# A fused state-space and convolution kernel: two turned tiles moved to ScalarE, five steps reordered, and the last tile read in halves

## The chip, the cores and the metric

The kernel runs on one core of a Trainium2 chip. A core has five engines with an instruction queue each: TensorE (PE in the profile; its weight loads are PEld), VectorE (DVE), ScalarE (ACT), GpSimd (POOL) and SyncE (SP), which here only issues DMAs. GpSimd issues the accumulating DMAs ("sums"). The metric is the device time of one execution in microseconds. Before the change the median of three runs is 385.52 us (384.85 to 386.91); the profiled execution took 384.57 us.

## The reference

The output is g * a + (1 - g) * b for 2048 rows and 1024 columns, with a gate g for each row.

```
g = sigmoid((x * gate_w).sum(-1))
# a: a diagonal complex state space, P = 1024 states
dt = exp(log_dt);  Lam_bar = exp(dt * Lam)
Bu = einsum("bld,pd->blp", x, ((Lam_bar - 1) / Lam)[:, None] * Bmat)
h[t] = Lam_bar * h[t - 1] + Bu[t]
a = 2 * einsum("blp,dp->bld", h, Cmat).real + x * Dskip
# b: a 4-tap filter on k, times v, then a causal convolution over all 2048 rows, by FFT
kv = shift_filter(k, shift_k) * v
b = x * (causal_conv(kv, ssm_k) + kv * ssm_D)
```

## The kernel before, in words

All instructions of an engine stay in the order in which the Python code issues them (put, line 92), so the text of the kernel is the schedule of each queue. Generators are used to interleave: a step of a generator issues its next few instructions on all engines, and the code below the definitions decides when each step comes. Nearly every operation is recorded under line 94, the line of put, so instructions are told apart by the tiles that they write and read.

The work has two halves. First the convolution b, in eight blocks of 128 channels: filter taps by matmuls (taps, line 562), a forward transform of the kernel (fwd_K, 628, tiles psk to Kh or BT) and of the data (fwd_V, 651, psv to Vh) by matmuls with cosine and sine tables, products on VectorE (products, 664; tiles G, wkh, t), and an inverse transform (inverse, 716, psz to cv) that is stored to DRAM (cv_scr). PSUM is a pool of four tiles of two banks each (line 81), and ScalarE evacuates most of them. The inverse tables SI and CI are made from angles: inverse_angles (378) on VectorE, then inverse_table (389), which is an Abs and two Sin on ScalarE. The rates of the states are made by state_params (411): its second step computes abv, rv (an Exp on ScalarE), thn and nthn; its third step the small tiles up to invden; its fourth step needs Sin. Exp and Sin lie in different tables of ScalarE, and each change shows as an ACT_TABLE_LOAD. Lines 1077 to 1120 order this start.

Second the state space a, in four blocks of 512 rows (tb) and four groups of 256 states (g). Bu (783) multiplies x by B (PE tile both, odd or even), ScalarE evacuates it to U, turn_U (872) adds a rotated part by a scaling on ScalarE (tile Q) and a sum by DMA (U<-Q), scan (891) runs the recurrence on VectorE, and Cy_g (1010) multiplies the states hb and U by C into the PSUM tile psy, eight matmuls for a row tile and group. B and C come transposed by DMA (load_BT 245, load_CT 1124), x too (load_xT 250, two halves of 0.5 MB).

C has eight tiles CT[0] to CT[7] of 128 states. Each must be turned by complex factors (turn_C, 1274): two scalings of the swapped parts on ScalarE (into m or, for tiles 4 and 5, into two tiles of the pool Q), two scalings in place, and the sum of both. For tiles 0 and 1 all four scalings are on ScalarE and the sum is two accumulating DMAs; for 4 and 5 the in-place scalings are on VectorE and the sums are DMAs (CT<-Q); for 2, 3, 6 and 7 the sum too is on VectorE. The pool Q has four buffers (line 1337), shared by turn_C and turn_U: a buffer is free again when its sum has landed.

Lines 1382 to 1480 are the schedule of the second half, in sixteen steps j, one for each scan: plan[j] names the units of matmuls that follow scan j ("B9 B10", "C0" and so on). In Bu_next (1365) after each of a unit's two B tiles up to two entries of the list on_act are stepped as fillers; they hold steps of turn_C:

```
for t in turning[2 * j:2 * j + 2]:
    run(t)
on_act += [lambda t=t: step(t) for t in turning[2 * j + 2:2 * j + 4] for _ in range(2)]
```

At j = 1 run finishes tiles 2 and 3 before the fillers that were put in for them at j = 0 are used, and B9 and B10 then have eight places for fillers: four that do nothing and four for tiles 4 and 5. At the end of step 1 scale_b (999) makes row tile 0's share of b on ScalarE (pbb, gd) and sums them by DMA; it needs the loads of row tile 0 (loads, 978) and the row Dskip (rows_).

The transposed loads of the second half are issued by SP in this order: CT[0], BT(2), CT[1], CT[2] (lines 1241 to 1248), BT(3), CT[3] (1295 to 1297), x's last block (1327, into the buffer that block 0 had, so behind the matmuls of Bu(7)), the stores of the last inverse, CT[4], CT[5], loads(0), the row Dskip, CT[6], CT[7], loads(1), loads(2) (1346 to 1353).

The end is lines 1482 to 1500: the last four row tiles get their last group's matmuls one after another, and finish (1043) scales each by the gate, adds xr and stores it. For the last row tile Cy_g sorts its eight matmuls by half, and finish reads and stores it in two halves on VectorE, both behind the eight.

Of the kernel before, what the change touches and what calls it, by code (L numbers as in the profile page):

```python
# [20 lines left out]
def kernel(  # L21
# [985 lines left out]
        act(gd, rows_, func=ACT.Identity, scale=gcols[:, t_:t_ + 1])  # L1007
        gather(pbb, gd)

    def Cy_g(tb, tl, ps, g, last):  # L1010
        X = hbs[tb, g] if tl < 2 else Us[tb, g][1]
        tsl = slice(tl % 2 * 128, tl % 2 * 128 + 128)
        steps_ = [(j, c, dh) for j in range(2) for c in range(2) for dh in range(2)]
        if tb * 4 + tl == NT - 1:
            steps_.sort(key=lambda s_: s_[2])
        for j, c, dh in steps_:
            mm(ps[dh], X[:, c, j, tsl], CT[2 * g + j][:, c, dh * 512:(dh + 1) * 512],
               g == 0 and j == 0 and c == 0, last and j == 1 and c == 1)

# [23 lines left out]
    def finish(t_, ps=None):  # L1043

        rows = rows_of(of, t_)
        product(t_)
        xr = ios.pop(t_)[1]
        if ps is None:
            yield
            ga = gas.pop(t_)  # L1050
            tt(ga, ga, xr, ALU.add)
        else:
            yield
            ga = a_room(t_)
            for o, i in ps:
                put("dve", V.scalar_tensor_tensor, out=ga[:, o], in0=i, scalar=gcols[:, t_:t_ + 1], in1=xr[:, o],
                    op0=ALU.mult, op1=ALU.add)
                if len(ps) > 1:
                    move(rows[:, o], ga[:, o])
            if len(ps) > 1:  # L1060
                return
        move(rows, ga)


    def step(gen):
        next(gen, None)

    def run(gen):
        for _ in gen:
            pass  # L1070
# [27 lines left out]
    step(sp)  # L1098
    run(first)
    dg1 = dgs(1, True)  # L1100
    run(angles)
    load("kT", 1)
    load("v", 1)
    load("kn", 1)
    fwd_K(0, (0, 1))
    fwd_V(0, (0, 1))
    step(sp)
    step(turns)
    taps(1, dg1)
    step(sp)  # L1110
    step(turns)
    p0 = products(0, 0)
    steps(p0, 3)
    tv = times_v(1)
# [17 lines left out]
    for c in range(NC - 1):  # L1132
        n, nn = c + 1, c + 2
        if c == 0:
            load("kn", 2)
            load("kT", 2)
            load("v", 2)
            load_BT(0, 0)
            load_xT(0, (0,))
            p1 = products(0, 1)  # L1140
            fwd_K(n, (0, 1))
            step(p0)
            run(tv)
            dg = dgs(nn, True)
            steps(p1, 2)
            step(p0)
            step(p1)
            run(p0)
            taps(nn, dg)
            step(sp)  # L1150
            fwd_K(n, (2, 3))
            step(p1)
            step(sp)
            fwd_V(n)
            run(p1)
            run(fold_K(nn))
            tv = times_v(nn)
            step(tv)
            load("kn", 3)
            load("kT", 3)  # L1160
            load_BT(0, 1)
            apart = spread(3)
            step(apart)
            load_xT(0, (1,))
            run(apart)
            lam_diag(0, lam_pool, True)
            continue
        if c == 6:
            put("pool", nc.gpsimd.tensor_copy, stamp, xTs[2][:, 0, 0:HB + 1:HB])
        tabs, back, prod = turn_table(c - 1) if c <= NG else none, inverse(c - 1), products(c)  # L1170
        step(old)
        step(tabs)
        if c == 6:
            step(parts)
        step(back)
        step(tv)
        steps(prod, 3)
        run(tv)
        step(old)
        step(tabs)  # L1180
        run(back)
        run(old)
        fk = none
        if nn < NC:
            dg = dgs(nn)
            if by_channel(nn):
                fk = fold_columns(nn)
                step(fk)
        if c == 2:
            step(parts)  # L1190
        fwd_K(n, (0, 1))
        if c in (2, 6):
            step(parts)
        fwd_K(n, (2, 3))
        if c == 4:
            step(parts)
        if c == 6:
            run(sp)
            s5p["Q"] = s5p["wu"]
            run(turns_U[2])  # L1200
            gate(0)
        step(prod)
        if nn < NC:
            if not by_channel(nn):
                fk = mirror_K(nn)
            step(fk)
            if c < 5:
                step(fk)
            if c == 4:
                step(parts)  # L1210
            if c == 1:
                load_BT(1, 0, True)
            elif c < 5:
                load("v", nn, True)
            step(parts)
            taps(nn, dg)
            if c == 5:
                load("v", nn)
                load_xT(2, held=True)
            if nn + 1 < NC:  # L1220
                load("kT", nn + 1, True)
                load("kn", nn + 1)
                apart = spread(nn + 1)
                step(apart)
                if c == 1:
                    load_BT(1, 1)
                elif c in (2, 3):
                    load_xT(1, (3 - c,))
                run(apart)
        step(prod)  # L1230
        run(fk)
        if n == NC - 1:
            overlap_K(n)
        run(prod)
        if nn < NC:
            tv = times_v(nn)
            step(tv)
            step(parts)
        else:
            run(next(tiles))  # L1240
            for pi in range(3):
                CT[pi] = ld.tile([128, 2, D], BF16, name="CTa", tag="ld")
                if pi == 0:
                    hold(CT[0][:, 0, 0:1])
                load_CT(pi)
                if pi == 0:
                    load_BT(2, 0)
                    load_BT(2, 1)
            run(next(tiles))
            run(next(tiles))  # L1250
        fwd_V(n, (0, 1))
        if c < 6 and c != 4:
            step(parts)
            if c in (1, 3):
                step(parts)
        fwd_V(n, (2, 3))
        if c in (4, 5):
            step(parts)
        if c == 1:
            lam_diag(1, lam_pool)  # L1260
        old = tabs
# [12 lines left out]
    def turn_C(pi):  # L1274
        by_sum = pi in (0, 1, 4, 5)
        if pi in (4, 5):
            m = [s5p["Q"].tile([128, D], BF16, name="Q") for c in range(2)]
        else:
            whole_m = m_pool.tile([128, 2, D], BF16, name="m")
            m = [whole_m[:, c] for c in range(2)]  # L1280
        for c in range(2):
            act(m[c], CT[pi][:, 1 - c], func=ACT.Identity, scale=mc2i[:, pi:pi + 1])
            yield
        for c, f in enumerate((c2r, mc2r)):
            if pi < 2:
                act(CT[pi][:, c], CT[pi][:, c], func=ACT.Identity, scale=f[:, pi:pi + 1])
            else:
                ts(CT[pi][:, c], CT[pi][:, c], f[:, pi:pi + 1], None, ALU.mult)
            if by_sum:
                gather(CT[pi][:, c], m[c])  # L1290
        if not by_sum:
            tt(CT[pi], CT[pi], whole_m, ALU.add)

    turning = [turn_C(pi) for pi in range(NP)]
    load_BT(3, 0)
    load_BT(3, 1)
    load_CT(3)
    with tc.tile_pool(name="fin", bufs=1, side="right") as fin:

        count = iter(range(16))  # L1300

        def room(shape, dt, name):
            return fin.tile(shape, dt, name=name, tag=f"fin{next(count)}")

        prod, back = products(c, 0, room, False), inverse(c - 1)
        run(old)
        steps(prod, 3)
        run(turns_U[3])
        run(next(tiles))
        steps(turning[0], 2)  # L1310
        step(back)
        steps(turning[1], 2)
        run(back)
        gate(1)
        gate(2)
        steps(prod, 2)
        b6, b7 = Bu(6)
        run(b6)
        run(b7)
        run(turns_U[6])  # L1320
        run(turning[0])
        run(turning[1])
        run(prod)
        b8, b9 = Bu(7)
        run(b8)
        run(b9)
        load_xT(3)
        b10, b11 = Bu(8)
        run(b10)
        run(b11)  # L1330
# [14 lines left out]
    CT_pool(range(4, NP), "ctb")  # L1345
    load_CT(4)
    load_CT(5)
    loads(0)
    move(rows_, bc(A_Dskip.rearrange("(o d) -> o d", o=1), [128, D]))
    load_CT(6)  # L1350
# [82 lines left out]
    for j in range(NS):  # L1433
# [6 lines left out]
        advance(j)  # L1440
        for t in turning[2 * j:2 * j + 2]:
            run(t)
        on_act += [lambda t=t: step(t) for t in turning[2 * j + 2:2 * j + 4] for _ in range(2)]
        turn = turns_U[turned[j]] if j in turned else none
        if j != 10 and plan[j][0:1] != "G":
            step(turn)
# [47 lines left out]
        fins.append(finish(t0 + tl, None if tl == 1 else pss[tl][1]))  # L1494
        step(fins[tl])
    for tl in range(4):
        Cy_g(tb, tl, pss[tl][0], NG - 1, True)
        if tl == 1:
            scale_a(t0 + tl, pss[tl][1])
        run(fins[tl])  # L1500
# [28 lines left out]
```

## Time and profile before

| | |
|---|---|
| median of the runs | 385.52 us (384.85 to 386.91) |
| profiled execution | 384.57 us |
| its span, first to last instruction | 382.8 us |
| TensorE clock granted | 0.998 |
| ScalarE busy | 303.6 us (79%) |
| transposing and plain DMA queue (q1) | 45.64 MB, 55.4% of the 16 DMA engines |
| queue of the sums (q0) | 25.17 MB, 38.9% |

Times in the profile are microseconds from the start of the span. A row of a timeline gives the start, the time, the engine, the line, the operation, the tiles out<-in, the shapes and the count; in brackets stands how long the engine was idle before it and what ended that. The sums by stretch give the length of the stretch, then busy time and number of instructions of PE, PEld, DVE, ACT and POOL, the granted clock, the DMA engines' mean busy share and GB/s. A row of the chain of waits gives a start, a time and the work (or DMA, or "issue") that the later work waited for.

### The profile page before, as it was taken

What the parts mean: (1) busy time and instruction counts of PE and PEld (TensorE: products, weight loads), DVE (VectorE), ACT (ScalarE), POOL (GpSimd) and SP (SyncE); (2) the same over time, 40 slices, a digit from 0 to 9 for tenths busy, and PEclk for the clock granted to TensorE, in tenths of its full rate; (3) what the DMA queues carried; (4) which work ended last, traced back from release to release, by engine and by line L of the source; (5) the groups of instructions that cost most, each with busy time, mean ns of one, the idle gap of its engine ahead of it and who ended that gap; (6) DMA issues with size and microseconds to landing.
All of it is one profiled execution on the core that took longest, in us unless ns stands there. A gap on an engine that the chain in (4) does not pass through costs nothing.

```text
span 382.8 us, 6633 instructions
## 1 busy us (share of the span) xinstructions
PE 371.3 (97%) x2419; PEld 198.3 (52%) x2453; DVE 371.2 (97%) x599; ACT 303.6 (79%) x469; POOL 81.8 (21%) x108
## 2 busy tenths in 40 slices
PE   7899999999999999999999999989999999999995
PEld 5566458575584846744454444434444444444442
DVE  7999999999999999999999999999999999999996
ACT  5898998988979999786979699675989759937601
POOL 4011030020301102031003110413414323634100
PEclk9999999999999999999999999999999999999999
DMA  7979999998999997959999999986899999898903
GB/s 166 165 108 223 218 205 205 245 203 211 201 164 211 208 213 169 198 125 154 192 221 164 226 203 250 213 153 125 150 222 192 208 245 246 136 250 156 238 8 110
DMA packets 126402, 71.77 MB, mean 187 GB/s; under 512 B 104665, under 2 KB 107489, under 8 KB 126370
## 3 DMA queue, kind: packets, MB, share of 16 engines
q1 hardware_dynamic: 111232, 45.64, 55.4%
q0 software_dynamic: 12976, 25.17, 38.9%
q10 hardware_dynamic: 2162, 0.54, 0.8%
q8 instruction: 19, 0.31, 0.3%
q14 instruction: 13, 0.11, 0.1%
HBM read 15.48 MB, written 8.39 MB: 62 GB/s over the span
## 4 chain that ended last, share of the span: by engine, by line
PE 52%; DVE 30%; issue 9%; DMA 4%; ACT 3%; ACTq 1%; POOL 0%; DVEq 0%; POOLq 0%
PE psy L94 29%; PE both L94 15%; DVE BT L94 11%; DVE wkh L94 8%; DVE G L94 5%; DVE t L94 3%; PE psz L94 2%; DVE ks L94 2%; PE psk L94 2%; DMA CT<-Q 2%; DMA pbb<-cv_scr 1%; PE psv L94 1%; DMA rows<-in_gate_w_dram 1%; PE p L94 1%; PE taps L94 1%
## 5 line engine op out<-in xcount | busy, mean ns | idle before, releaser
L94 PEld LDWEIGHTS <-BT 128*128 128x128 bf16 x640 | 62.0, 98 | 48.3 <-issue 0.2
L94 PE MATMUL both<-xT,BT 128*128 128x512 bf16 x375 | 83.0, 379 | 0.4
L94 POOL DMA_DIRECT2D U<-Q x26 | 26.7, 1039 | 88.8 <-ACT Q L94 31.0
L94 PEld LDWEIGHTS <-hb 128*128 128x128 bf16 x256 | 24.9, 98 | 31.4 <-issue 1.6
L94 PEld LDWEIGHTS <-U 128*128 128x128 bf16 x240 | 23.5, 98 | 28.3
L94 PE MATMUL psy<-CT,hb 128*128 128x512 bf16 x157 | 36.3, 379 | 0.1
L94 ACT ACTIVATE Vh<-psv 128x1024 bf16<-128x1024 f32 x32 | 30.7, 1034 | 5.3 <-PE psv L94 5.3
L94 PE MATMUL psy<-CT,U 128*128 128x512 bf16 x149 | 34.6, 379 | 0.2
L94 ACT ACTIVATE Q<-U,lam 128x512 bf16<-128x512 bf16 (+1 forms) x52 | 29.9, 612 | 4.9 <-DMA CT<-Q 4.9
L94 DVE TENSOR_TENSOR_SCAN W<-rv,init,A 128x256 bf16<-128x256 f32 x48 | 32.2, 730 | 0.0
L94 POOL DMA_DIRECT2D G<-wkh x8 | 9.7, 1218 | 102.8 <-DVE wkh L94 102.8
L94 ACT ACTIVATE U<-both 128x512 bf16<-128x512 f32 x44 | 24.1, 595 | 8.0 <-PE both L94 7.5
L94 PEld LDWEIGHTS <-SF 128*128 128x128 bf16 x184 | 18.0, 98 | 19.7 <-issue 1.4
L94 PE MATMUL psk<-eok,SF 128*128 128x512 bf16 (+1 forms) x119 | 27.9, 354 | 0.3
L94 PE MATMUL psz<-G,CI 128*128 128x512 bf16 x64 | 24.3, 379 | 0.1
L94 PE MATMUL psz<-G,SI 128*128 128x512 bf16 x64 | 24.3, 379 | 0.0
L94 PE MATMUL psy<-CTa,hb 128*128 128x512 bf16 x94 | 22.6, 379 | 1.2 <-ACT U L94 1.0
L94 PE MATMUL taps<-dg,kT 128*128 128x128 bf16 (+1 forms) x352 | 21.7, 210 | 0.8 <-DMA kT<-in_B_k_dram 0.8
L94 PEld LDWEIGHTS <-kT 128*128 128x128 bf16 x352 | 21.0, 100 | 2.5 <-DMA kT<-in_B_k_dram 2.1
L94 DVE TENSOR_TENSOR wkh<-BT,Vh 128x3072 bf16<-128x3072 bf16 (+4 forms) x20 | 21.8, 1110 | 0.0
L94 DVE TENSOR_TENSOR wkh<-Kh,Vh 128x3072 bf16<-128x3072 bf16 (+2 forms) x16 | 21.2, 1348 | 0.0
L94 PE MATMUL psy<-CTa,U 128*128 128x512 bf16 x87 | 20.4, 379 | 0.1
(227 smaller groups left out, 846.1 us busy)
## 6 DMA issues: line engine op xcount, KB each, us to landing
U<-Q POOLq DMA_DIRECT2D x26, 256.0 KB, 5.3
G<-wkh POOLq DMA_DIRECT2D x6, 768.0 KB, 8.8
cv_scr<-cv SPq DMA_DIRECT2D x16, 256.0 KB, 5.7
kn<-in_B_ssm_k_dram SPq DMA_DIRECT2D x5, 512.0 KB, 4.0
v<-in_B_v_dram SPq DMA_DIRECT2D x5, 512.0 KB, 6.2
out_dram<-m SPq DMA_DIRECT2D x8, 256.0 KB, 4.5
BT<-cv_scr SPq DMA_DIRECT2D x7, 256.0 KB, 5.9
out_dram<-BT SPq DMA_DIRECT2D x7, 256.0 KB, 2.0
```

What stands on the lines that cost most here:

```text
L94: i = f(*a, **kw)
```

## The change

- Tiles 4 and 5 of C: the in-place scalings go from VectorE to ScalarE, with a step after each; the list of fillers leaves out the entries at j = 0 and has four a tile at j = 1.
- Rates sooner: state_params' second step comes before the inverse angles, which come after the first quarter of fwd_K. Inverse sine later: one step of inverse_table is left out where it stood, and the run further down issues it with the cosine.
- BT(3) is issued ahead of CT[2].
- x's last block is issued after CT[5] instead of after Bu(7).
- Last tile in halves: four matmuls of a half, then the read of that half. The first half is scaled by ScalarE and added by VectorE, the second read by VectorE as before.

```diff
-    def Cy_g(tb, tl, ps, g, last):
+    def Cy_g(tb, tl, ps, g, last, halves=(0, 1)):
         X = hbs[tb, g] if tl < 2 else Us[tb, g][1]
         tsl = slice(tl % 2 * 128, tl % 2 * 128 + 128)
-        steps_ = [(j, c, dh) for j in range(2) for c in range(2) for dh in range(2)]
-        if tb * 4 + tl == NT - 1:
-            steps_.sort(key=lambda s_: s_[2])
-        for j, c, dh in steps_:
+        for j, c, dh in [(j, c, dh) for j in range(2) for c in range(2) for dh in halves]:
             mm(ps[dh], X[:, c, j, tsl], CT[2 * g + j][:, c, dh * 512:(dh + 1) * 512],
                g == 0 and j == 0 and c == 0, last and j == 1 and c == 1)
...
-            for o, i in ps:
-                put("dve", V.scalar_tensor_tensor, out=ga[:, o], in0=i, scalar=gcols[:, t_:t_ + 1], in1=xr[:, o],
-                    op0=ALU.mult, op1=ALU.add)
+            for h, (o, i) in enumerate(ps):
+                if len(ps) > 1:
+                    Cy_g(tb, 3, [x for _, x in ps], NG - 1, True, (h,))
+                if len(ps) > 1 and h == 0:
+                    act(ga[:, o], i, func=ACT.Identity, scale=gcols[:, t_:t_ + 1])
+                    tt(ga[:, o], ga[:, o], xr[:, o], ALU.add)
+                else:
+                    put("dve", V.scalar_tensor_tensor, out=ga[:, o], in0=i, scalar=gcols[:, t_:t_ + 1], in1=xr[:, o],
+                        op0=ALU.mult, op1=ALU.add)
                 if len(ps) > 1:
                     move(rows[:, o], ga[:, o])
...
-    run(angles)
     load("kT", 1)
     load("v", 1)
     load("kn", 1)
-    fwd_K(0, (0, 1))
+    fwd_K(0, (0,))
+    step(sp)
+    run(angles)
+    fwd_K(0, (1,))
     fwd_V(0, (0, 1))
-    step(sp)
     step(turns)
     taps(1, dg1)
     step(sp)
-    step(turns)
     p0 = products(0, 0)
...
-            for pi in range(3):
+            for pi in range(2):
                 CT[pi] = ld.tile([128, 2, D], BF16, name="CTa", tag="ld")
...
         for c, f in enumerate((c2r, mc2r)):
-            if pi < 2:
+            if by_sum:
                 act(CT[pi][:, c], CT[pi][:, c], func=ACT.Identity, scale=f[:, pi:pi + 1])
             else:
                 ts(CT[pi][:, c], CT[pi][:, c], f[:, pi:pi + 1], None, ALU.mult)
             if by_sum:
                 gather(CT[pi][:, c], m[c])
+                yield
...
     load_BT(3, 0)
     load_BT(3, 1)
+    CT[2] = ld.tile([128, 2, D], BF16, name="CTa", tag="ld")
+    load_CT(2)
     load_CT(3)
...
         run(b9)
-        load_xT(3)
         b10, b11 = Bu(8)
...
     load_CT(4)
     load_CT(5)
+    load_xT(3)
     loads(0)
...
-        on_act += [lambda t=t: step(t) for t in turning[2 * j + 2:2 * j + 4] for _ in range(2)]
+        if j > 0:
+            on_act += [lambda t=t: step(t) for t in turning[2 * j + 2:2 * j + 4] for _ in range(4 if j == 1 else 2)]
...
     for tl in range(4):
-        Cy_g(tb, tl, pss[tl][0], NG - 1, True)
+        if tl < 3:
+            Cy_g(tb, tl, pss[tl][0], NG - 1, True)
         if tl == 1:
             scale_a(t0 + tl, pss[tl][1])
         run(fins[tl])
```

## The prediction

> **What bounds the kernel now.** I read the page first, then the sums by stretch, then the waits and the chain of the stretch that the change touches most, and then timelines of single engines. Durations are those of the profiled execution: 384.57 us, of which 382.8 are its span. The runs shown have a median of 385.52, which is 0.95 us more; savings are subtracted from that median.
>
> ```profile
> PE 371.3 (97%) x2419; PEld 198.3 (52%) x2453; DVE 371.2 (97%) x599; ACT 303.6 (79%) x469; POOL 81.8 (21%) x108
> ```
>
> PE and DVE are both busy 97% of the time, so no engine has room to win much; a gain must be time in which PE stands still. The sums by stretch (length, then busy time by engine) say where that can be:
>
> ```profile
> 13.00:34.00 21.00, 20.22 (x155) 11.59 (x156) 19.22 (x39) 19.93 (x23) 1.45 (x2) 1.00 0.91 159
> 34.00:164.00 130.00, 128.46 (x1088) 81.58 (x1096) 129.41 (x125) 115.06 (x179) 16.63 (x21) 1.00 1.05 204
> 164.00:253.00 89.00, 87.31 (x481) 40.89 (x491) 88.10 (x139) 74.05 (x125) 19.97 (x22) 1.00 1.03 196
> 253.00:379.00 126.00, 124.80 (x596) 57.04 (x607) 123.50 (x275) 87.56 (x135) 39.26 (x46) 1.00 0.85 174
> ```
>
> From 34 to 164 DVE has no free time, and the chain runs on it; from 164 on PE sets the pace. The DMA share (second number from the end) is at 1 up to 253: the DMA engines are full too. PE's one large stop behind 164 is at 253, and the chain shows whose it is:
>
> ```profile
> 244.74 5.78 DMA CT<-Q
> ...
> 251.17 0.71 ACT Q L94
> ...
> 252.51 0.60 ACT U L94
> ...
> 253.15 2.97 PE psy L94 x13
> ```
>
> ScalarE stood still for 4.92 us before its Q at 250.54, because the pool Q has four buffers and all four were in the turning of C's tiles 4 and 5, whose sums (CT<-Q) were issued only at 244.74, behind DVE's scaling of these tiles (it ended at 244.45). So ScalarE emptied B's PSUM tiles late, and C's first row found no PSUM tile until 253.11. The last matmul before it started at 251.73 and the spacing is 0.22: PE lost 253.15 - 251.95 = 1.20 us.
>
> **The start (rates sooner, inverse sine later).** DVE waits once here:
>
> ```profile
> 19.86 0.18 DVE L94 TENSOR_TENSOR abv<-pcol 128x16 f32<-128x16 f32 x1 [1.05 <-ACT rv L94]
> ```
>
> With the rates ahead of the angles, abv stands at 16.3 and ScalarE takes rv (0.22) in its gap of 0.49 before 16.88, so the wait of 1.05 goes. What is late next: the products at 20.39 need Vh, whose evacuation ends at 19.74, so DVE gains 0.63; then ks at 23.48 needs ScalarE's evacuation of the taps, which starts at 22.18 and takes 1.02, so of the 0.63 only 23.48 - 23.23 = 0.25 are left. From there DVE runs without a gap over 0.32 up to PE's wait for it at 47.79, so PE gets the 0.25 there. The moved sine (table load 1.28 and SI 1.06) no longer stands before the evacuations at 25.48; these 2.34 us now stand behind Vh, before Kh at 32.84. PSUM has four tiles, and PE needs the first of Kh's again at 36.71; it is then free at about 34.2 + 1.0 = 35.2. Cover 1.5 us, cost 0. Bounds 0 (the tap load of kT, landed 33.08, is behind a full DMA) to 0.63. I take **0.25**.
>
> **BT(3) ahead of CT(2).** SP issues BT(3) at 193.28, behind two transposes of CT(2) that take 2.75. It lands at 199.58 and 201.55, and Bu(7) needs the halves at 200.14 and 201.87: a margin of 0.32, which the 0.25 from the start nearly uses up; the swap gives 2.7 more. CT(2) comes some 5 us later than 195.8; its first reader is ScalarE at 221.36. Cost 0, bound 0.25 (the gain kept).
>
> **Tiles 4 and 5 by ScalarE.** DVE loses four scalings, which run from 243.96 to 245.55: 1.59 us. After 189 no wait of PE for DVE over 0.15 us is shown before the last half tile, so this gains nothing by itself. ScalarE gets four operations spaced 1.04 (the like CTa<-CTa at 204.45 to 208.61): 4.16. The turning starts one B block earlier, at B9: before, B9's four fillers went to generators (tiles 2 and 3) that had already been run out. The sums then go out at about 231 to 239 instead of 244.7 to 247, and the wait of 4.92 goes. ScalarE is gapless from 217.6 to 245.53 but for 0.14 at 231.49, so I move its rows: 245.53 - 0.25 - 0.14 + 4.16 = 249.30, two Q 1.24, the ends 0.23, and B's tile in 1.09: 251.86. PE could go on at 251.95 - 0.25 = 251.70. So C's first row would start at 251.90 instead of 253.15: **1.25 with the start's 0.25**, if every load is there in time.
>
> **x's last block later.** That is the doubtful part. Before, x's two transposes went out at 207.25 and 208.63 and landed at 212.4 and 218.9 (the trace's semaphore events). Now 1.05 MB stand between CT(5) and all that follows on SP's queue: row 0's loads, Dskip's rows, CT(6), CT(7) and loads(1), (2). That queue is full just there:
>
> ```profile
> DMA packets 13239, 5.52 MB, mean 221 GB/s; under 512 B 11997, under 2 KB 11997, under 8 KB 13237
> ...
> q1 hardware_dynamic: 12701, 4.53, 86.8%
> q0 software_dynamic: 536, 0.97, 21.5%
> ```
>
> This is 219 to 244. CT(5) landed at 229.6; without x beside them the sums before it end sooner, and I put it at 228.6 (an estimate: some 0.2 MB of backlog at 219 gone). At 0.221 MB/us x lands at 233.4 to 236; B needs it at 237.9: no stop. But the sums of tile 4 now run beside the loads from 232.5. In 208 to 216 x's transposes ran beside sums too, and got two thirds:
>
> ```profile
> q1 hardware_dynamic: 4117, 1.05, 67.4%
> q0 software_dynamic: 276, 0.53, 38.6%
> ```
>
> Two thirds of 0.221 are 0.147 MB/us: by this x lands at 233.8, the 0.79 MB of row 0 and Dskip at 239.1 (needed 239.6), CT(6) at 242.7 (needed 241.8), CT(7) at 246.3 (needed 245.1 plus what was waited). ScalarE, in order, has B's evacuations behind these reads: 1.15 us of the 1.25 would be given back. Plain loads ran faster than transposes (0.29 MB/us in 230 to 234); by that row all come in time and nothing is given back. At 0.131 MB/us, the rate of 208 to 216 itself, 2.5 are given back. I take 0.6, the middle of the first two, and keep 0 and 2.5. Net: 1.25 - 0.6 = **0.65**.
>
> [...]
>
> **Last tile in halves.** PE's order stays. Before, both halves were read after all eight matmuls:
>
> ```profile
> 378.62 1.41 DVE L94 SCALAR_TENSOR_TENSOR BT<-psy,gcols,xlast 128x512 bf16<-128x512 f32 x2 [0.42 <-PE psy L94]
> ```
>
> PE counted up its semaphore once, with the eighth (at 378.59); the fourth of them ended at 377.72. With the read written behind four matmuls ScalarE, idle since 376.3, takes half 0 from 377.75 to 378.40 (0.65: the 0.60 of U<-both, 128x512 out of PSUM, and a little for the scale, as 1.11 stands to Vh's 1.03), DVE adds xr (0.42) until 378.82, and half 1 follows at once: 0.74, end 379.50 instead of 380.03. The last store goes out 0.54 earlier and takes the same 1.84. Bounds: 0.54 gained, 0.15 lost if PE's second half had to wait for ScalarE's read (378.42 + 0.88 + 0.90 = 380.20). I take **0.54**.
>
> Sum: 0.65 + 0.54 = 1.19, that is 383.4 for an execution like the profiled one and 385.52 - 1.19 = **384.3** on the median.
>
> **Rivals.** (1) *All loads in time*: 1.25 + 0.54, and the last 0.2 up to PE's own limit, 2.0: **383.5**. For it: plain loads' rate; x no longer beside the sums of 208 to 220. Against: the full DMA. (2) *Slower: the sums go ahead of the transposes.* Whenever a sum (q0) has work, the transposes stand still. The 0.52 MB of tile 4 take 2.8 us at 0.19 MB/us (the sums alone, 216 to 220), then tile 5 and row 0's sum 4.2 more, all ahead of CT(6): it lands at 245.7, 3.8 us after ScalarE wants it, and C's first row starts at 255.7. That is 1.25 - 3.8 + 0.54 = -2.0: **387.5**. It decides from CT(7) landing at 246.9 on, where the change is worth nothing. Against it: the two thirds above. [...] (3) *The halves don't part*: 0.65 - 0.15 = 0.5: **385.0**.
>
> **How the numbers follow.** Chances: forecast 0.45, rival 1 0.27, rival 2 0.18, rival 3 0.10. A difference of 0.5% (1.93 us) is about what can be told from no change. Only rival 1 reaches 383.6: faster 0.27. Rival 2 lies on the other bound, 387.45; with the runs' own spread two thirds of it count: slower 0.12. The rest, 0.61, is within. Range: from 383.5 less 0.6 of spread, 382.9, to 387.0, which leaves out half of rival 2.
>
> **What would show it.** Right: ScalarE's wait of 4.9 for Q is gone; C's first row starts between 251.7 and 252.7; DVE's 1.05 at 19.86 is gone and ks starts at 23.2; DVE's last operation starts some 0.2 us after the last matmul's end instead of 0.7 and ends 0.9 after it instead of 1.45. Wrong: waits of ScalarE for CT transposes at 242 to 249, a PE stop before B's block 12 near 238, or PE waiting for ScalarE between the last halves.

## The result, and the profile after

The changed kernel takes **388.6 us** (median of 14 runs, 385.84 to 392.08) against 385.01 for the kernel before on the same chip (14 runs): a ratio of 1.0077 with a 95% interval of 1.0052 to 1.0103. Ratios, intervals and counts of runs, here and below, leave out runs that are over 1.5% longer than the fastest of their kernel (here the one of 392.08), and a ratio is not the quotient of the two medians. It is slower, and it lies outside the range of the prediction (384.3; 382.9 to 387.0). The profiled execution took 386.75 us (span 385.0), which is 2.2 more than that of before.

The page's busy times, and the sums by stretch with the same limits as before:

```profile
PE 374.1 (97%) x2453; PEld 199.5 (52%) x2453; DVE 369.7 (96%) x595; ACT 309.3 (80%) x474; POOL 81.4 (21%) x108
```

```profile
164.00:253.00 89.00, 87.17 (x488) 40.47 (x486) 87.64 (x139) 75.54 (x124) 18.43 (x21) 1.00 1.00 190
253.00:379.00 126.00, 124.00 (x603) 56.59 (x603) 120.12 (x269) 90.02 (x139) 40.63 (x47) 1.00 0.85 176
```

DVE has 1.5 us less of work than before (371.2), as planned, and yet it is idle for longer: from 253 on it works 120.12 of 126 us instead of 123.50. In both stretches PE does less than before in the same time. So PE has stopped somewhere, and VectorE waits behind it. The chain of waits shows where (start, duration, what):

```profile
234.89 3.04 SPq L94
237.94 0.04 issue
237.98 6.88 DMA CT<-in_A_C_im_dram
...
244.95 0.07 ACT m L94
...
252.50 1.23 ACT Q L94 x2
...
254.36 0.60 ACT U L94
254.96 0.04 issue
255.00 7.07 PE psy L94 x32
```

Read it upwards from PE: C's first row (psy, 255.00) waited for ScalarE's evacuation U; that stood behind ScalarE's Q, and ScalarE as a whole behind m, the turning of C's tile 6, which waited for a transposed load that was 6.88 us under way. Before, this place of the chain held the sums CT<-Q. ScalarE's timeline has the waits in brackets:

```profile
238.96 1.15 ACT L94 ACTIVATE pbb<-pbb,omg 128x1024 bf16<-128x1024 bf16 x1 [1.25 <-DMA pbb<-cv_scr]
240.34 1.15 ACT L94 ACTIVATE gd<-rows,gcols 128x1024 bf16<-128x1024 bf16 x1 [0.24 <-DMA rows<-in_A_Dskip_dram]
...
244.95 2.19 ACT L94 ACTIVATE m<-CT,mc2i 128x1024 bf16<-128x1024 bf16 x2 [2.23 <-DMA CT<-in_A_C_im_dram]
```

These are 3.72 us in all, and each is a load that stands behind x's last block on SP's queue. The wait of 4.92 for Q is gone, but the new waits no longer lie in idle time.

The difference of 2.2 us between the two profiled executions has three parts. PE waits for ks at 46.71 instead of 47.79: 1.07 gained at the start. Beyond the spacing of its matmuls PE loses 0.97 at 248.40 and 3.15 at 255.00, where it lost 1.20 before: 2.92 lost. The last tile, from the end that PE would have had without its last stop to the last landing, takes 3.65 instead of 3.32: 0.33 lost. -1.07 + 2.92 + 0.33 = 2.18.

### The profile page after: what moved, and what is told of

It is laid out like the page before. It is cut to its first block, busy times and chain, and to the rows that moved or that the text cites. A ratio compares the mean times of both kernels' runs of the same rounds, so it can differ in the third digit from the quotient of the medians.

```text
span 385.0 us, 6664 instructions
## 1 busy us (share of the span) xinstructions
PE 374.1 (97%) x2453; PEld 199.5 (52%) x2453; DVE 369.7 (96%) x595; ACT 309.3 (80%) x474; POOL 81.4 (21%) x108
## 4 chain that ended last, share of the span: by engine, by line
PE 52%; DVE 32%; issue 5%; ACT 3%; DMA 3%; SPq 3%; ACTq 1%
PE psy L94 29%; PE both L94 15%; DVE BT L94 12%; DVE wkh L94 9%; DVE G L94 5%; SPq L94 3%; DVE t L94 3%; PE psz L94 2%; DVE ks L94 2%; DMA CT<-in_A_C_im_dram 2%; PE psk L94 2%; PE psv L94 1%; DMA rows<-in_gate_w_dram 1%; DVE ev L94 1%; PE p L94 1%
## 5 line engine op out<-in xcount | busy, mean ns | idle before, releaser
L94 PE MATMUL taps<-dg,kT 128*128 128x128 bf16 (+1 forms) x352 | 22.9, 216 | 0.0
L94 PEld LDWEIGHTS <-kT 128*128 128x128 bf16 x352 | 22.2, 103 | 1.2 <-DMA kT<-in_B_k_dram 0.7
L94 ACT ACTIVATE BT<-psy,gcols 128x1024 bf16<-128x1024 f32 (+1 forms) x6 | 6.3, 1044 | 20.0 <-PE psy L94 20.0
```

What stands on the lines that cost most here:

```text
L94: i = f(*a, **kw)
```

## The experiments

Every kernel ran beside runs of the kernel before on the same chip, and its ratio is against those: 384.96 us was their median for x's place and the tail as before, 385.72 for the start alone, C's tiles and the first kernel with two PSUM tiles, 385.82 for the start with the swap, the second of these and three added operations, 385.29 for one and two added operations.

### Which part costs: x's place and the tail

**x's last block back at its old place**, all else as changed:

```
         run(b9)
+        load_xT(3)
         b10, b11 = Bu(8)
...
     load_CT(5)
-    load_xT(3)
     loads(0)
```

> The changed kernel with x's last block loaded at its old place, behind B's block 7; everything else of the change stays. Theory 1 (the loads behind x on SP's queue come late, and ScalarE, which takes its work in order, stands still for them): ScalarE's waits of 1.25 and 2.23 us for row 0's sum and for CT(6) are gone, TensorE's stop at C's first row falls from 4.1 us to at most 0.5, and the profiled execution takes 382.6 to 383.6 instead of 386.75; the granted clock of the timed runs is back at 0.998 in nearly all. Theory 2 (ScalarE is late by its own 4.2 us of added scaling): it has no such waits any more, yet empties B's tiles as late as before, C's first row stays at 254 to 255 and the time at 386 or more. Either way the last half tile still waits for ScalarE's read, by about 0.8.

383.14 us, ratio 0.9953 (0.9929 to 0.9977). That is theory 1: faster than the kernel before. In ScalarE's timeline the same operations stand without brackets; C's first row starts without a stop.

```profile
237.55 1.13 ACT L94 ACTIVATE pbb<-pbb,omg 128x1024 bf16<-128x1024 bf16 x1
238.59 1.13 ACT L94 ACTIVATE gd<-rows,gcols 128x1024 bf16<-128x1024 bf16 x1
...
240.83 2.19 ACT L94 ACTIVATE m<-CT,mc2i 128x1024 bf16<-128x1024 bf16 x2
```

Theory 2 falls with it: ScalarE has the same 4.2 us of added work here and is not late.

**The tail back, and both back.** finish, Cy_g and the last loop as before, once with x late and once with x at its old place:

```
-        for j, c, dh in [(j, c, dh) for j in range(2) for c in range(2) for dh in halves]:
+        steps_ = [(j, c, dh) for j in range(2) for c in range(2) for dh in range(2)]
+        if tb * 4 + tl == NT - 1:
+            steps_.sort(key=lambda s_: s_[2])
+        for j, c, dh in steps_:
...
-        if tl < 3:
-            Cy_g(tb, tl, pss[tl][0], NG - 1, True)
+        Cy_g(tb, tl, pss[tl][0], NG - 1, True)
```

> The changed kernel with the last tile's end as before (all eight matmuls, then two halves by VectorE). If the halves cost what the trace shows, 0.33 us from the last matmul's unstalled end to the last landing, the profiled execution takes 386.2 to 386.6 and TensorE's stop of 0.8 at 380.4 is gone, while the stops of 1.0 and 3.2 at 248 and 255 stay; the median falls by 0.2 to 0.5 against the changed kernel. If the halves save something after all (VectorE ends sooner after the last matmul), it is 0.3 to 0.5 slower than the changed kernel.

> The changed kernel with both taken back, x's place and the last tile's end. By theory 1, and a tail that costs 0.33: 382.3 to 383.2, the fastest of these, 0.3 under the one with x alone back. By theory 2: 386 or more.

With the tail alone back 386.68 us, ratio 1.0048 (1.0029 to 1.0066); with both back 383.23, ratio 0.9956 (0.9940 to 0.9971). The stop before the last four matmuls is gone in both. From the start of the last matmul, less the stop, to the last landing the run with x alone back takes 3.87 and the one with both back 3.70: the changed tail costs 0.2 to 0.3 in a trace, and the two medians (383.14 and 383.23) cannot tell them apart. The tail is the small part, x's place the large one. Against the changed kernel the tail's return gained more than the expected 0.2 to 0.5 on the median; in that trace x's second half landed 2.9 us sooner than in the changed kernel's (233.7 against 236.5), and PE's stop at C's first row was 2.74 instead of 0.97 and 3.15: a draw of the DMAs, that is a difference between one execution and the next, and nothing to do with the tail.

**x late alone**, on the kernel before:

```
         run(b9)
-        load_xT(3)
         b10, b11 = Bu(8)
...
     load_CT(5)
+    load_xT(3)
     loads(0)
```

> The kernel before with x's last block loaded behind CT(5), and nothing else. Theory 1: ScalarE waits for the loads behind x, C's first row starts at 255 to 257 instead of 253.1, and the time is 387 to 389, with a granted clock of the runs below 0.996 where TensorE's stop is over 3 us. Theory 2: no effect without ScalarE's added work, 384 to 385.5.

385.06 us, ratio 1.0000 (0.9982 to 1.0019). Theory 1 as I had put it fails here: the loads are late, and it costs nothing. (Its profiled execution took 386.28, but that one has a wait of PE of 2.1 us for another DMA, ks<-lo, at 157.51.) ScalarE's timeline shows why:

```profile
238.74 1.15 ACT L94 ACTIVATE pbb<-pbb,omg 128x1024 bf16<-128x1024 bf16 x1 [2.53 <-DMA pbb<-cv_scr]
240.08 1.15 ACT L94 ACTIVATE gd<-rows,gcols 128x1024 bf16<-128x1024 bf16 x1 [0.19 <-DMA rows<-in_A_Dskip_dram]
...
246.60 2.19 ACT L94 ACTIVATE m<-CT,mc2i 128x1024 bf16<-128x1024 bf16 x2 [0.86 <-DMA CT<-in_A_C_im_dram]
...
249.35 1.15 ACT L94 ACTIVATE pbb<-pbb,omg 128x1024 bf16<-128x1024 bf16 x1 [0.56 <-DMA pbb<-cv_scr]
...
252.22 1.34 ACT L94 ACTIVATE Q<-U,lam 128x512 bf16<-128x512 bf16 x2 [0.68 <-DMA CT<-Q]
```

The waits for late loads add up to 4.14, and the wait for Q has shrunk from 4.92 to 0.68: 4.82 in all. They have used up the idle time that stood in front of Q, and nothing more. So it is the pair that costs: C's tiles on ScalarE fill this idle time with work, and x's late block needs it as slack.

### The parts alone, and the pair

**C's tiles 4 and 5 by ScalarE alone**, and **the same with x late**, on the kernel before:

```
-            if pi < 2:
+            if by_sum:
                 act(CT[pi][:, c], CT[pi][:, c], func=ACT.Identity, scale=f[:, pi:pi + 1])
...
                 gather(CT[pi][:, c], m[c])
+                yield
...
-        on_act += [lambda t=t: step(t) for t in turning[2 * j + 2:2 * j + 4] for _ in range(2)]
+        if j > 0:
+            on_act += [lambda t=t: step(t) for t in turning[2 * j + 2:2 * j + 4] for _ in range(4 if j == 1 else 2)]
```

> The kernel before with C's tiles 4 and 5 turned by ScalarE one block earlier, and nothing else; x's last block stays at its old place. Theory: ScalarE's wait of 4.92 us for Q goes, its 4.2 us of added work takes that room, no load comes late, and TensorE's stop of 1.20 at C's first row goes: 0.9 to 1.3 us under the kernel before. Rival (ScalarE is late by its own work): the stop stays at 1.2 or grows, same time as the kernel before or slower.

> The kernel before with both, C's tiles 4 and 5 by ScalarE and x's last block behind CT(5). Alone, x's place cost nothing (the waits of 4.0 us for late loads stood inside ScalarE's idle 4.92), and C's tiles alone should gain about 1. Theory (the two collide: without that idle time every wait for a late load is added to ScalarE's own work, and tile 5's sums run beside CT(6)'s loads): TensorE stops for 2.5 to 4.5 us at C's first row, 2 to 4 us slower than the kernel before, and the granted clock falls to 0.993 to 0.995 in part of the runs. Rival (the two add up, and what made the changed kernel slow lies in the swap or the start): 1 us faster than the kernel before.

C's tiles alone: 385.6 us, ratio 0.9990 (0.9962 to 1.0018). The times of these runs are too wide (383.21 to 400.52) to show 1 us; the trace shows no wait of ScalarE from 228 to 256 and none of PE from 190 to 260, and its span is 381.8 (before: 382.8), as expected. With x late as well: 391.14 us, ratio 1.0123 (1.0081 to 1.0165), and the stop at C's first row is back. This view lists PE's waits of 190 to 262 (us in total, times, longest):

```profile
PE both L94 <- DMA BT<-in_A_B_re_dram: 2.8, 1, 2.8
PE psy L94 <- ACT U L94: 2.7, 1, 2.7
```

The second line is the collision, without start, swap or tail. The first is another thing, a late B tile; C's tiles alone, whose loads are the same up to there, have no such wait, so it is a draw. The profiled execution, 391.32, pays for both, and its clock was halved from 203.32 to 206.73, right at the end of the first, so the ratio does not say what the collision alone costs. The next two kernels are about the B tile.

**The start alone**, and **the start with BT(3) ahead of CT(2)**, on the kernel before:

```
-    run(angles)
...
-    fwd_K(0, (0, 1))
+    fwd_K(0, (0,))
+    step(sp)
+    run(angles)
+    fwd_K(0, (1,))
     fwd_V(0, (0, 1))
-    step(sp)
     step(turns)
     taps(1, dg1)
     step(sp)
-    step(turns)
```

```
-            for pi in range(3):
+            for pi in range(2):
...
     load_BT(3, 1)
+    CT[2] = ld.tile([128, 2, D], BF16, name="CTa", tag="ld")
+    load_CT(2)
     load_CT(3)
```

> The kernel before with the start's part alone (rates ahead of the angles, the second turn's step earlier, inverse sine behind the first half of K's forward transform). The changed kernel reached TensorE's wait for ks at 46.71 instead of 47.79, of which some 0.3 us came in with the first DMA landings. Theory: the start gives 0.77; the time is 0.5 to 1.0 us under the kernel before, and TensorE's wait for ks lies at 46.7 to 47.1. Rival: all of the 1.07 is a draw of the DMAs, and what the start gives is the 0.25 of the prediction or nothing: within 0.3 us of the kernel before.

> The kernel before with the start's part and BT(3) ahead of CT(2), nothing else. The start alone brought TensorE's wait for ks from 47.79 to 47.01, and then B's block 7 stopped for 0.8 and 0.3 us for BT(3), whose margin had been 0.32. Theory (the start gives 0.8, which holds to the end only where BT(3) comes sooner): no stop for BT(3) at 198 to 204, the stop of 1.2 at C's first row stays, 0.6 to 1.0 us under the kernel before. Rival (the swap is worth nothing, the stops of the start alone were a draw of the DMAs): as the start alone.

The start alone: 385.02 us, ratio 0.9970 (0.9931 to 1.0008). With the swap: 384.09, ratio 0.9967 (0.9935 to 0.9998). PE's wait for ks lies at 47.01 and 46.73; over the kernels with the new start whose trace has it, it lies between 46.60 and 47.01, over those with the old one between 47.68 and 48.12. So the start gives 0.8 to 1.1, and it is not a draw. The two ratios do not tell these two kernels apart; what the swap is worth has to come from the traces. With the start alone, though, PE waits for both halves of BT(3):

```profile
PE both L94 <- DMA BT<-in_A_B_im_dram: 0.8, 1, 0.8
PE both L94 <- DMA BT<-in_A_B_re_dram: 0.3, 1, 0.3
```

With the swap these waits are not there. The margin of BT(3) had been 0.32, and a start that is faster by 0.8 needs it to come sooner. One trace of each cannot rule out that a part of the wait is a draw (C's tiles with x late, with the old start, had it too), but in no trace with the swap has PE waited for a B tile.

### The tail

**Halves in two PSUM tiles.** On the kernel with x back, the second half of the last tile gets a PSUM tile of its own; as there is none free, it takes that of the first row tile, and its 12 earlier matmuls come behind the third tile's. In the second kernel VectorE's products of the last two rows are moved behind its read of that first tile as well:

```
+        else:
+            ps = ps2([128, 2, 512], "psy")
+            pss[3][0][1] = ps[:, 0]
+            pss[3][1].append((slice(512, D), ps[:, 0]))
+            for g in range(NG - 1):
+                Cy_g(tb, 3, pss[3][0], g, False, (1,))
...
-        step(fins[tl])
+        if tl < 2:
+            step(fins[tl])
...
         run(fins[tl])
+        if tl == 0:
+            step(fins[2])
+            step(fins[3])
```

> The changed kernel with x's last block back at its old place and the last tile's halves in two PSUM tiles instead of one; the second half's earlier matmuls follow the third tile's, since its PSUM tile comes free only then. Theory (TensorE waited for ScalarE's read of the other half only because both halves are one PSUM tile): the stop of 0.82 before the last four matmuls is gone, ScalarE's read lies beside them, and the time is 0.4 to 0.7 us under the run with x alone back, 0.3 to 0.5 under the one with both back. Rival (the two cannot work side by side in any case, or the order costs as much elsewhere): a stop of 0.5 or more stays in the last 8 us, and the time is that of the run with x alone back or longer.

> The run with the halves in two PSUM tiles, with VectorE's products of the last two output rows moved behind its read of the first tile, whose PSUM tile the second half takes. In the run before, TensorE stood still for 0.64 us for that read. Theory: this stop falls to 0.15 at most, the halves stay side by side, and the time from the last matmul's start to the last landing is 1.41 + 1.85 = 3.3 us instead of 3.7 with both back: 0.3 to 0.5 us under the run with both back, the fastest of all. Rival (the moved products only move the stop): same as the run with both back, or longer.

384.58 us, ratio 0.9978 (0.9958 to 0.9999), and 383.73, ratio 0.9945 (0.9914 to 0.9977). First the timeline of the changed kernel's end, then that of the second of these two:

```profile
379.65 0.69 ACT L94 ACTIVATE BT<-psy,gcols 128x512 bf16<-128x512 f32 x1 [1.52 <-PE psy L94]
380.37 0.42 DVE L94 TENSOR_TENSOR BT<-BT,xlast 128x512 bf16<-128x512 bf16 x1 [0.32 <-ACT BT L94]
380.39 1.02 PE L94 MATMUL psy<-CT,U 128*128 128x512 bf16 x4 [0.83 <-ACT BT L94]
...
381.45 0.75 DVE L94 SCALAR_TENSOR_TENSOR BT<-psy,gcols,xlast 128x512 bf16<-128x512 f32 x1 [0.66 <-PE psy L94]
```

```profile
375.59 2.75 PE L94 MATMUL psy<-CT,U 128*128 128x512 bf16 x12
...
377.57 0.69 ACT L94 ACTIVATE BT<-psy,gcols 128x512 bf16<-128x512 f32 x1 [4.12 <-PE psy L94]
378.29 0.43 DVE L94 TENSOR_TENSOR BT<-BT,xlast 128x512 bf16<-128x512 bf16 x1 [1.74 <-ACT BT L94]
378.63 0.74 DVE L94 SCALAR_TENSOR_TENSOR BT<-psy,gcols,xlast 128x512 bf16<-128x512 f32 x1
```

In the changed kernel PE's last four matmuls start only when ScalarE has read the other half (379.65 + 0.69). With two tiles the last twelve matmuls run through as one piece, ScalarE's read at 377.57 beside them, and VectorE's last read starts at 378.63. So it was the shared tile. In the first kernel a PE wait of 0.6 for VectorE's read of the first row tile takes the gain away again; the second has no PE wait at all from 240 on. From its last matmul's start to the last landing it takes 3.29, where the run with both back takes 3.70: the halves are worth 0.41. By its ratio it is the fastest kernel here, though the interval overlaps that of the one with both back.

### What the median has over the profiled execution

Of the 3.6 us between the medians the traces explain 2.2. The granted clock of the changed kernel's runs hinted at the rest: 8 of 13 had a mean of 0.995 or less. The trace of the run with the tail alone back caught it. The sums by stretch of that run, with PEclk third from the end:

```profile
252.00:253.00 1.00, 0.00 (x0) 0.00 (x0) 0.97 (x2) 0.97 (x4) 0.63 (x2) 1.00 1.34 275
253.00:254.00 1.00, 0.46 (x2) 0.19 (x2) 1.00 (x3) 1.00 (x4) 0.41 (x1) 0.79 1.06 264
254.00:255.00 1.00, 1.00 (x4) 0.37 (x3) 1.00 (x5) 1.00 (x4) 0.00 (x0) 0.50 1.09 197
...
256.00:257.00 1.00, 1.00 (x4) 0.41 (x3) 1.00 (x4) 1.00 (x3) 0.00 (x0) 0.50 0.18 35
257.00:258.00 1.00, 1.00 (x6) 0.44 (x5) 0.97 (x6) 1.00 (x2) 0.00 (x0) 1.00 0.00 0
```

PE stops until 253.5, and just as it starts again its clock is halved, until 257.0: 3.4 us, which cost it up to 1.7. Is the stop the cause? **ScalarE work added** to the kernel with both back delays C's first row without touching a load; Dskip's row for output row 1 is scaled four times (three times, twice) instead of once:

```
-        act(gd, rows_, func=ACT.Identity, scale=gcols[:, t_:t_ + 1])
+        for _ in range(4 if t_ == 1 else 1):
+            act(gd, rows_, func=ACT.Identity, scale=gcols[:, t_:t_ + 1])
         gather(pbb, gd)
```

> The run with both back, x's place and the last tile's end, with three more ScalarE operations (the scaling of Dskip's row for output row 1 written four times instead of once, with the same outcome), 3 x 1.04 = 3.1 us of work ahead of the evacuations that C's first row waits for; no load and no sum is moved. Theory (a stop of TensorE is paid twice: once as its length, and in part of the runs again by a half clock for 3.4 us behind it): TensorE stops 2.5 to 3.1 us at C's first row; profiled execution and median are 2.5 to 5 us over the run with both back, and the runs fall in two groups, one with a clock of 0.998 or more and one some 1.7 us longer with 0.993 to 0.995. Rival (the half clock comes from something else in the changed kernel, such as the load on the DMA engines or the late transposes): 2.5 to 3.1 us longer, with the clock at 0.997 or more in all runs.

> As the run with three added ScalarE operations, with one: the run with both back, and 1.04 us of ScalarE work with no effect on any load. In the run with both back TensorE's stop at C's first row is 0.06, so it should now be 1.0 to 1.1, as long as before the change (1.20). Theory (the clock falls only behind a stop that is long against 3.4 us): the clock is 0.997 or more in nearly all runs, and the time is 1.0 to 1.2 us over the run with both back. Rival (any stop does it): 0.993 to 0.995 in a good part of the runs, 2 us or more longer.

> The same with two added operations, 2.1 us. Theory: a stop of 2.0 to 2.2 us; 0.993 to 0.995 in some of the runs (less often than with three, where nine of ten had 0.995 or less), the others at 0.997 or more and only 2.1 us over the run with both back. Rival: the clock does not depend on the stop's length; the same share of runs as with one or with three.

Three added: 389.2 us, ratio 1.0077 (1.0043 to 1.0112). One: 383.95, ratio 0.9970 (0.9944 to 0.9996). Two: 386.32, ratio 1.0006 (0.9977 to 1.0036).

| kernel | PE's wait at C's first row in its trace | runs with a mean clock of 0.995 or less |
|---|---|---|
| both back | none | 0 of 6 |
| x alone back | none | 0 of 12 |
| C's tiles alone | none | 0 of 11 |
| the start alone | none (0.3 and 0.8 at B tiles) | 1 of 12 |
| halves in two tiles, first and second kernel | none | 2 of 11, 0 of 12 |
| the kernel before, beside these | 1.0 | 7 of 100 |
| the start with the swap | 1.1 | 1 of 12 |
| one operation added | 1.1 | 0 of 11 |
| x late alone | 1.4 | 0 of 12 |
| two added | 2.3 | 3 of 9 |
| tail alone back | 2.6 | 4 of 7 |
| C's tiles with x late | 2.7 (and 2.8 at a B tile) | 5 of 5 |
| three added | some 3 (added work; no trace of it) | 8 of 9 |
| the changed kernel | 0.8 (at a B tile) and 3.0 | 8 of 13 |

Up to a stop of 1.4 the lower clock is rare (11 of 199), from 2.3 on it is common (28 of 43), whether loads or ScalarE's own work cause the stop: that is the theory, and the rivals fall. The length is that of one trace of each kernel, and the few cases at the top are not explained by this stop. Two added operations lengthened the trace's stop to 2.3, and that execution too had its clock halved behind it. Where a kernel's runs have both kinds, those with the lower clock are longer by 1.2 (two added: 386.49 mean of the three at 0.994, against 385.34 of the six at 0.998 or more) or 1.3 (tail alone back). In the changed kernel it is 2.4: the five with the higher clock have a mean of 386.79, as its profiled execution (386.75), and the eight with the lower one 389.19. So the median's surplus lies in these eight; but 2.4 is more than the 1.7 that a half clock of 3.4 us can cost, and that longer stops in those runs are the rest is not shown.

Why only some runs have it is not shown. In the three traces with such a fall it comes at 253.59 (tail alone back), 254.12 (two added) and 203.32 (C's tiles with x late), behind stops of 2.6, 2.3 and 2.8 us, and the half clock ends at 257.0, 257.5 and 206.73, some 3.4 us later each time. The changed kernel's profiled execution had its stop of 3.0 and kept a granted clock of 1.00 from 250 to 258; that of x late alone had its wait of 2.1 at 157.51 and a mean clock of 1.000.

## Why the prediction was wrong, step by step

| term | predicted | measured | where |
|---|---|---|---|
| start | -0.25 | -1.07 (-0.78 alone) | PE's wait for ks |
| C's tiles by ScalarE | -1.00 | -1.14 | stop 1.20 to 0.06, both back |
| BT(3) ahead of CT(2) | 0 | 0 to -1.1 | waits for BT(3) of the start alone |
| x's last block later | +0.6 | +4.06 | 0.97 + 3.15 - 0.06 |
| last tile in halves | -0.54 | +0.33 | 3.32 to 3.65 |
| the clock behind a stop | not seen | some +1.4 | median over profiled: 1.85, before 0.44 |

**The step that failed** is the price of x's place: "In 208 to 216 x's transposes ran beside sums too, and got two thirds". That was an average over 8 us in which the two queues hardly ever moved at the same time. The same trace shows it in finer cuts. First 213 to 214 of the kernel before, then 216 to 219 (packets, MB, share of the engines' time):

```profile
q1 hardware_dynamic: 1121, 0.29, 127.5%
q0 software_dynamic: 1, 0.00, 0.1%
```

```profile
q0 software_dynamic: 340, 0.60, 110.7%
q1 hardware_dynamic: 43, 0.00, 2.1%
```

In 213 to 214 the transposes moved and the sums stood, though four sums had been issued from 208.60 on (with q1 idle a sum's bytes moved 1.4 us after its issue, as for the one of 258.48), and the first of them landed at 216.53. In 216 to 219 the sums moved and q1 stood: x's 1.05 MB had moved by then (the 1.05 of 208 to 216), but x's second half landed only at 218.9, near the end of these sums. Rival 2, in which transposes stand still whenever a sum has work, says the second of these and not the first; it was set aside with a chance of 0.18 by the average. In the changed kernel it was the sums that went first. Shown are 234 to 236, with x's last parts, row 0 and CT(6) on q1 and tile 4's sums on q0, then 243 to 244, with CT(6) not yet landed and CT(7) issued:

```profile
q0 software_dynamic: 206, 0.39, 108.7%
q1 hardware_dynamic: 89, 0.02, 5.8%
```

```profile
q0 software_dynamic: 101, 0.20, 108.4%
q1 hardware_dynamic: 7, 0.00, 1.0%
```

So x's second half landed at 236.5 instead of the forecast 233.8, row 0 and Dskip at 240.3 (239.1), CT(6) at 244.86 (242.7). x's place cost 4.06, outside the 0 to 2.5 that I had kept. Rival 2 had CT(6) at 245.7, C's first row at 255.7 and, in an execution like the profiled one, 386.6; it came out at 244.86, 255.00 and 386.75. Its order was not the whole of it here either: tile 5's sums were issued at 236.97 and 238.00, and from 237.5 to 240.5 q1 moved 0.81 MB and q0 nothing. What decides which queue goes first is open. In 234 to 236 the sums moved 0.39 of 0.41 MB, where I had left them a third.

The rates in the prediction do not set transposes below plain loads either: the transposes of 213 to 214 moved 0.29 MB in 1 us, and in 230 to 234, which gave the 0.29 for plain loads, 2604 of 2876 packets are under 512 B.

There was a second error in that step: that the loads ahead gain from x's leaving ("I put it at 228.6"). CT(5) did land at 228.72, but with x at its old place it landed at 229.16 (x alone back) and 228.61 (both back): little or nothing of this gain was x's. CT(4) is issued at 218 to 219 in either case. Without x the DMA engines have nothing to do just before it; the changed kernel's 208 to 218 in slices of 0.25 us:

```profile
GB/s 172 221 139 148 172 188 180 188 180 180 213 172 180 180 164 197 188 213 172 188 197 188 197 180 205 98 25 0 0 0 0 0 0 0 66 385 385 213 0 0
```

At its old place x had run where such a hole comes without it, at next to no cost to CT(5), and now it stood in a full stretch.

**The last tile** failed on its lower bound: I named the case that PE's second half waits for ScalarE's read, priced it at 0.15 lost (rival 3) and chose the other. It lost 0.33: from a standstill the four matmuls took 1.02 where I had 0.88, and the handovers the rest. What I had not read is that both halves are one PSUM tile.

**The start** was right up to ks (forecast 23.23; 23.22 with the start alone) and too small behind it: the bound of 0.63 did not reach. VectorE's wait of 0.32 at 29.91, which I took to stay, went as well, because the table load and SI (2.34 us) no longer held ScalarE up there. **C's tiles by ScalarE** were right in mechanism and size; once x is back, C's first row starts at 250.9, and the time, 383.14, is near what rival 1 gave for all loads in time (383.5). **The swap** was costed at nothing because its cover was enough for a gain of 0.25; with 0.8 it is, by the traces, what keeps that gain.

Of the signs named, the wait for Q and the wait at 19.86 went as forecast, and two of those for "wrong" came: ScalarE's wait for a transpose of CT at 244.95, and PE's for ScalarE between the last halves. What the median has on top of the traces, the clock, was in no rival.

## What to carry to other kernels

An engine's idle time in front of one wait is slack for every wait ahead of it in its queue (with x late alone late loads took 4.14 of ScalarE's 4.92 us, at a ratio of 1.0000); when a change fills that time with work, look for the loads that were late within it, and do not move a load behind them in the same change. A queue's share of the DMA engines must be read in cuts fine enough to show whether two queues share or one stands (67.4% and 38.6% over the 8 us of 208 to 216, 127.5% and 0.1% in the 1 us of 213 to 214), and a load is cheapest where the engines would stand, as x's was at its old place (383.14 against 388.6). Stops of TensorE of 2.3 us or more came with a lower clock in 28 of 43 runs here, stops of up to 1.4 in 11 of 199, and such runs were longer by 1.2 (two added) and 1.3 (tail alone back); so the gap that a change closes or opens can count for more than its length.

## What the runs showed of the hardware that was not expected

The queue of the transposes and that of the sums went one at a time: 1121 packets against 1 in 213 to 214 of the kernel before, 7 against 101 in 243 to 244 of the changed one. A transpose whose bytes have moved can still land late behind the other queue's sums (x's second half before: moved by 216, landed at 218.9). A half clock of 3.4 us came with stops of 2.3 to 2.8 us in three traces, at or just behind their end.

One execution of the kernel with three added operations took 1386.38 us: its matmuls of B took 1103 ns on average instead of 380, the others of their shape as long, from the first to the last, while VectorE's work took 372.7 us as always. The trace has no record of the granted clock for it. What put TensorE into this pace is open; it occurred once in all these runs.
